# Second FFN product: from float32r pairs to plain float32 in two chunks and float16 pairs in ten

## The chip, the cores and the metric

The kernel runs on one core of one Trainium2 chip. The metric is device microseconds of one execution. Engines: TensorE (PE, with its weight loads PEld), VectorE (DVE), ScalarE (ACT), GpSimd (POOL), and SyncE (SP), whose queue issues all transfers here.

## The reference, cut to what matters

A local attention with block summaries feeds a feed-forward network (FFN):

```python
# q, k, v: (4, 8, 768, 64) float
k_sum = k.reshape(B, H, nb, 32, D).max(axis=3); v_sum = ....mean(axis=3)
scores_l = scale * q @ k^T, kept where |i - j| < 16
scores_s = scale * q @ k_sum^T + log(32)
a = softmax(concat(scores_l, scores_s))
x = a @ concat(v, v_sum)            # as (3072 tokens, 512)
h = x @ w_in                        # 512 -> 2048
g = h / (1 + exp(-h))
out = g @ w_out                     # 2048 -> 512, 3072 x 512
```

The inputs arrive as 64-bit floats; the kernel gets the weights as pairs of 32-bit words and makes float32 of them itself.

## The kernel before, in words

**Tiling.** The 3072 tokens are 24 stages of 128 (attention, six for each of four batch entries) and 12 chunks of 256 (FFN). The FFN's hidden dimension of 2048 is 8 weight pairs (`fp`) of 256. One item is one chunk with one weight pair: first product (`ffn1`, L749), 24 float16 matmuls of 128x256 (x and w_in are each a high and a low float16, three of the four cross products are taken); `tanh` (L761) and a gate (L762); then `g` is split into `gh` (L763) and `gl` (L764, in helper L228); then the second product (`ffn2`, L756), 2 halves of 6 matmuls of 128x512, in float32r (also high and low, three cross products). Chunks 0 and 1 run first, interleaved over the weight pairs: chunk 0 pairs 0 to 3, chunk 1 pairs 0 to 7, chunk 0 pairs 4 to 7. Chunks 2 to 11 follow in order with all eight pairs each.

**Weights** (`job_w`, L672). There are 16 weight tiles of 1 MB in memory (8 pairs, `kind` 0 is w_in, `kind` 1 is w_out), each loaded once by L681 into its own buffer `wr`, in which early attention data lie before. ScalarE takes the upper words (L689) into a staging buffer `raw`, ScalarE or VectorE prepares the lower words (L685, L687), VectorE joins them (L691, into `raw`). For `kind` 0 a maximum (L696), two tiny matmuls (L700, L701) and L704 give a power-of-two scale `u` and its inverse `r`. Then a scaled high half (L720, in helper L218) and the low remainder (L722, in helper L225) are written, float16 for w_in and float32r for w_out. `asc` combines the weight scale with the scale of v for the `tanh`.

**Scale of v** (`v_scale`, L408). Per batch entry, ScalarE sums absolute values (L436; L513 for the first), VectorE adds these up (`am_sum`, L405), and the largest of 128 partitions becomes a power of two.

**Attention.** For each stage four head groups: scores (L575 plain float32 for the first batch entry, L577 and L578 float16 later), softmax, the probabilities as float16 pairs `p` (L624), a transposing transfer (L627), and the product with v (L656); the first two stages run in plain float32 (L609 to L641). `job_mean` makes the block means with plain float32 matmuls (L509). `job_x` (L669, L670) writes x as `xh` and `xl`.

**Order.** All of this is handed to a planner (`Plan`), which has a cost for each operation on each engine that can run it, latencies and due times (`prio`, with offsets from `TUNE`). It simulates the engines, picks engine and order, and the kernel issues instructions in that order; each engine works through its list in order. While TensorE has nothing to do before the FFN starts, the plan puts filler matmuls (L312) there.

Of the kernel before, what the change touches and what calls it, by code (L numbers as in the profile page):

```python
# [19 lines left out]
DM, DFF = 512, 2048  # L20
# [30 lines left out]
NSUP = 2  # L51

# [151 lines left out]
def local_attn_ffn(ctx: ExitStack, tc: tile.TileContext, qkT, qF, qD, kF, kD, v, vR, w, out):  # L204
# [33 lines left out]
    wt = {}  # L238
    wr = [wp.tile([P, 2, DM, 2], U32, name="wt") for _ in range(2 * NFP)] if wide else None
# [9 lines left out]
    nc.vector.memset(spread, 2.0 ** -13)  # L249
# [7 lines left out]
    asc_t = [const.tile([P, NFP], F32, name=f"asc{i}") for i in range(2)]  # L257

# [48 lines left out]
    gh_t = ring(NG, [P, 2 * CH], F32R, "gh")  # L307
    gl_t = ring(NG, [P, 2 * CH], F32R, "gl")
# [96 lines left out]
    def am_sum(n, prio):  # L405
        plan.op({"dve": 73}, lambda e: nc.vector.tensor_reduce(out=am_t[:, 7:8], in_=am_t[:, :n], axis=AX.X, op=ALU.add), r=[("am", j) for j in range(n)], w=["am4"], prio=prio)

    def v_scale(b, prio):  # L408
# [7 lines left out]
            lambda e: nc.vector.tensor_scalar(out=sc2[:, 1:2], in0=sc2[:, 1:2], scalar1=2.0 ** -14, scalar2=None, op0=ALU.mult),  # L416
# [7 lines left out]
        if b:  # L424
            plan.op({"pool": 250, "dve": 150}, lambda e: times(e, asc_t[b % 2], ur_t[:, :, 0], vsc_t[b % 2][:, 1:2]),
                    r=[("vsc", b % 2)] + [("ur", f) for f in range(NFP)], w=[("asc", b % 2, f) for f in range(NFP)], prio=prio)

    def job_v(b, prio):
        prio += nudge("v", b)
        for j in range(4):  # L430
# [5 lines left out]
            plan.op({"act": 830}, lambda e, vr=vr, j=j: nc.scalar.activation(out=vr, in_=vr, func=AF.Abs, accum_out=am_t[:, j:j + 1]), r=[("vm", j)], w=key + [("am", j)], prio=prio)  # L436
# [60 lines left out]
    def job_mean(prio):  # L497
        prio += nudge("mean")
        k = sbank()
        for t in range(NTILE):  # L500
# [10 lines left out]
            if NPL < NTILE:  # L511
                junk, jk = pinned()
                plan.op({"act": 612}, lambda e, src=src, t=t, junk=junk: nc.scalar.activation(out=junk[:, :DM], in_=src, func=AF.Abs, accum_out=am_t[:, t:t + 1]), r=key, w=jk[:1] + [("am", t)], prio=prio)  # L513
# [41 lines left out]
    def job_a(m, prio):  # L555
# [24 lines left out]
        plan.op({"pe": 640 if b == 0 else 330}, scores, r=[(x, s % 2, hp) for x in ("qk", "qkm") for hp, _ in heads(g)] + ([("qkk", s % 2)] if b else []), w=[("bank", k)], prio=prio, cols=728)  # L580
# [91 lines left out]
    def job_w(fp, kind, prio):  # L672
        prio += nudge("w", fp, kind)
        (wf, key), src = low_staging(), w[fp, kind]
        mine = [("w", f, kind) for f in (2 * fp, 2 * fp + 1)]
        if wide:
            rt = wr[2 * fp + kind].rearrange("p j c i -> p (j c) i")
            low, top = rt[:, :, 0], rt[:, :, 1]
            wu = wf.bitcast(U32)
            sides = [k + x for k in mine for x in ((0,), (1,), (0, "side"), (1, "side"))]  # L680
            plan.op({"dma": 3300}, lambda e: nc.sync.dma_start(out=rt.rearrange("p c i -> p (c i)"), in_=src.bitcast(U32)), w=mine + sides, prio=prio - TUNE["w_dma"] + nudge("wd", fp, kind))  # L681
# [7 lines left out]
            plan.op({"act": 1000}, lambda e: nc.scalar.activation(out=wf, in_=top.bitcast(F32), func=AF.Prelu, scale=REBIAS, alpha=-SIGN), r=mine, w=key, prio=prio)  # L689
            plan.op({"act": 1000, "dve": 610}, last_bits, r=mine, w=[("wb", fp, kind)], prio=prio)  # L690
            plan.op({"dve": 1140}, lambda e: nc.vector.scalar_tensor_tensor(out=wu, in0=wu, scalar=3, in1=low, op0=ALU.logical_shift_left, op1=ALU.bitwise_or), r=mine + [("wb", fp, kind)], w=key, prio=prio)  # L691
        else:
            plan.op({"dma": 1650}, lambda e: nc.sync.dma_start(out=wf, in_=src), w=key + mine, prio=prio)
        u, r = ur_t[:, fp, 0:1], ur_t[:, fp, 1:2]
        if kind == 0:
            plan.op({"dve": 1160}, lambda e: nc.vector.tensor_reduce(out=wm_t[:, fp:fp + 1], in_=wf, axis=AX.X, op=ALU.max, apply_absolute_value=True), r=key, w=[("wm", fp)], prio=prio, port=())  # L696
            k = sbank()

            def gather(e):
                nc.tensor.matmul(out=bank[k][:, :2], lhsT=spread, rhs=wm_t[:, fp:fp + 1].to_broadcast([P, 2]), start=True, stop=False)  # L700
                nc.tensor.matmul(out=bank[k][:, :2], lhsT=spread, rhs=least.to_broadcast([P, 2]), start=False, stop=True)  # L701

            plan.op({"pe": 240}, gather, r=[("wm", fp)], w=[("bank", k)], prio=prio, cols=2)
            plan.op({"dve": 170}, lambda e: nc.vector.scalar_tensor_tensor(out=ur_t[:, fp, :].bitcast(U32), in0=bank[k][:, :2].bitcast(U32), scalar=0x7F800000, in1=flip, op0=ALU.bitwise_and, op1=ALU.bitwise_xor),  # L704
                    r=[("bank", k)], w=[("ur", fp)], prio=prio, port=())
            plan.op({"pool": 250, "dve": 130}, lambda e: times(e, asc_t[0][:, fp:fp + 1], u, vsc_t[0][:, 1:2]), r=[("ur", fp), ("vsc", 0)], w=[("asc", 0, fp)], prio=prio)
        by = u if kind else r

        def flat(part):
            return wt[fp, kind][:, part].rearrange("p j c -> p (j c)")  # L710

        def hi(e):
# [21 lines left out]
    def job_f(i, c, f):  # L734
# [30 lines left out]
        for u in range(2):  # L765
            plan.op({"pe": 1380}, ffn2(u), r=[("gh", n), ("gl", n), have[1], have[3], ("wl", f, 1)], w=[("bank", ob[u])] + ([("turn", i)] if u else []), prio=late, cols=3072)
# [151 lines left out]
```

## Time and profile before

| | |
|---|---|
| median of the runs | 668.44 us (667.22, 668.44, 670.69) |
| profiled execution | 665.93 us, span 664.1 us |
| TensorE busy | 643.0 us, 97% of the span |
| VectorE, ScalarE, GpSimd busy | 470.9, 409.0, 208.9 us |
| granted TensorE clock | 0.997 |
| TensorE, L749 (both forms) | 2304 matmuls |
| TensorE, L756 (both forms) | 1152 matmuls |
| moved by DMA | 97.39 MB, mean 147 GB/s |

The span runs from the first to the last instruction of the profiled execution; the execution's own time is 1.8 us longer. Matmuls overlap in the record, so the mean of one matmul's length is not its price: the price is the distance from start to start. In the rows, `bank<-wt,gh 128*128 128x512` means: PSUM tile `bank`, written from `wt` and `gh`, a stationary 128x128 against a moving 128x512.

### The profile page before, as it was taken

The page shows a single profiled execution, that of the slowest core. Times are in us where ns is not written, and L with a number is a line of the kernel's source. Part 1 is how long each engine was busy: PE and PEld are TensorE (multiplying, and loading weights), DVE is VectorE, ACT ScalarE, POOL GpSimd, SP SyncE. Part 2 cuts the span into 40 slices and gives each one's busy share as a digit, 9 for nine tenths or more (in the row PEclk, how much of TensorE's full clock was granted, in tenths as well). Part 3 has the DMA queues.
Part 4 walks back from the last instruction along what each step waited for, and adds up shares of the span by engine and source line. Part 5 has one row for each costly group of instructions (what it writes and reads, how often), then busy time and mean ns, then how long its engine had stood idle before and what let it go on. Part 6 is the DMA issues. An engine that isn't in the chain of part 4 may idle for free. (4 is left out here: it accounts for less than half of the span.)

```text
span 664.1 us, 13776 instructions
## 1 busy us (share of the span) xinstructions
PE 643.0 (97%) x5032; PEld 513.5 (77%) x5032; DVE 470.9 (71%) x1354; ACT 409.0 (62%) x892; POOL 208.9 (31%) x218
## 2 busy tenths in 40 slices
PE   7999799998999999999999999999999999999997
PEld 2667578776887888878887887887788888888886
DVE  5998778768679975778898955598883658843221
ACT  5898697766577665567665754467863647533222
POOL 3025565313543352124246123233442332100000
PEclk9999899999999999999999999999999999999999
DMA  8697871687564785465764764256663352310000
GB/s 285 247 327 226 315 277 56 156 203 192 140 145 120 171 210 170 112 163 121 194 134 121 198 171 148 69 149 148 157 181 98 91 133 42 78 37 13 33 1 32
DMA packets 99239, 97.39 MB, mean 147 GB/s; under 512 B 76887, under 2 KB 79959, under 8 KB 97123
## 3 DMA queue, kind: packets, MB, share of 16 engines
q1 hardware_dynamic: 99170, 96.51, 53.0%
q8 instruction: 39, 0.64, 0.4%
q14 instruction: 30, 0.24, 0.1%
HBM read 70.34 MB, written 6.29 MB: 115 GB/s over the span
## 5 line engine op out<-in xcount | busy, mean ns | idle before, releaser
L749 PE MATMUL bank<-xh,wt 128*128 128x256 f16 x1536 | 272.8, 274 | 2.3 <-DVE wt L225 2.0
L749 PEld LDWEIGHTS <-wt 128*128 128x128 f16 x2304 | 218.3, 98 | 51.1 <-issue 23.7
L756 PE MATMUL bank<-wt,gh 128*128 128x512 f32 x768 | 249.8, 406 | 0.3 <-ACT gh L763 0.3
L749 PE MATMUL bank<-xl,wt 128*128 128x256 f16 x768 | 210.1, 274 | 0.0
L756 PE MATMUL bank<-wt,gl 128*128 128x512 f32 x384 | 152.0, 396 | 4.7 <-POOL gl L228 4.6
L756 PEld LDWEIGHTS bank<-wt,gh 128*128 128x128 f32 x768 | 134.8, 189 | 25.5 <-issue 0.8
L228 POOL TENSOR_TENSOR gl<-t,gh 128x512 fp32r<-128x512 f32 x59 | 86.3, 1463 | 187.9 <-ACT gh L763 154.6
L762 DVE SCALAR_TENSOR_TENSOR t<-t,bank 128x512 f32<-128x512 f32 x96 | 65.6, 683 | 73.8 <-ACT t L761 73.3
L761 ACT ACTIVATE t<-bank,asc 128x512 f32<-128x512 f32 x96 | 65.3, 682 | 83.0 <-PE bank L749 82.6
L624 DVE SCALAR_TENSOR_TENSOR p<-e,sum,p 128x128 f16<-128x128 f32 x352 | 101.6, 350 | 6.7 <-ACT p L596 4.3
L585 ACT ACTIVATE e<-e,mx 128x182 f32<-128x182 f32 x192 | 83.7, 437 | 26.8 <-DVE mx L582 26.5
L756 PEld LDWEIGHTS bank<-wt,gl 128*128 128x128 f32 x384 | 72.0, 188 | 24.5 <-POOL gl L228 8.0
L763 ACT CAST gh<-t 128x512 fp32r<-128x512 f32 x96 | 58.9, 614 | 37.5 <-DVE t L762 35.0
L582 DVE CUSTOM_DVE_ANT_0 e<-bank,masks,qsc 128x182 f32<-128x182 f32 x144 | 52.8, 400 | 19.1 <-PE bank L578 18.8
L598 POOL TENSOR_SCALAR p<-e,sum 128x182 f16<-128x182 f32 x66 | 30.7, 471 | 112.7 <-DVE sum L591 55.9
L228 POOL TENSOR_TENSOR vv<-raw,vv 128x1024 f16<-128x1024 f32 x19 | 42.0, 2211 | 12.3 <-ACT vv L210 10.1
L228 DVE TENSOR_TENSOR gl<-t,gh 128x512 fp32r<-128x512 f32 x37 | 31.9, 863 | 17.0 <-ACT gh L763 16.6
L596 ACT ACTIVATE p<-e,sum 128x182 f16<-128x182 f32 x74 | 30.5, 439 | 19.9 <-DVE sum L591 9.5
L585 ACT ACTIVATION_READ_ACCUMULATOR e<-e,mx 128x1 f32 x192 | 36.1, 188 | 0.0
L481 DVE SCALAR_TENSOR_TENSOR qk<-raw,qsc,qk 64x1264 f16<-64x1264 f32 x18 | 30.1, 1669 | 6.9 <-ACT qk L480 6.4
L656 PEld LDWEIGHTS <-vv 128*64 128x64 f16 x880 | 25.6, 110 | 6.2 <-issue 4.8
L480 ACT ACTIVATE qk<-raw,qsc 128x1264 f16<-128x1264 f32 x18 | 24.2, 1343 | 8.9 <-DMA raw<-in_kD_dram 8.9
(133 smaller groups left out, 685.9 us busy)
## 6 DMA issues: line engine op xcount, KB each, us to landing
wt<-in_w_dram SPq DMA_DIRECT2D x16, 1024.0 KB
raw<-in_kD_dram SPq DMA_DIRECT2D x18, 632.0 KB
raw<-in_v_dram SPq DMA_DIRECT2D x20, 512.0 KB
raw<-in_qD_dram SPq DMA_DIRECT2D x18, 512.0 KB
out_dram<-raw SPq DMA_DIRECT2D x24, 256.0 KB
raw<-in_kF_dram SPq DMA_DIRECT2D x12, 384.0 KB
raw<-in_qF_dram SPq DMA_DIRECT2D x9, 512.0 KB
raw<-in_vR_dram SPq DMA_DIRECT2D x12, 384.0 KB
```

Source lines behind the costliest of these rows:

```text
L228: eng[e].tensor_tensor(out=out, in0=in0, in1=in1, op=ALU.subtract)
L481: plan.op({"dve": 1450}, lambda e: nc.vector.scalar_tensor_tensor(out=kst[64:, :, :NLOC], in0=kr[64:], scalar=qs[64:, 1:2], in1=kst[64:, : ...
L582: plan.op({"dve": 258 if b == 0 else 323}, lambda e, i=i: nc.vector.tensor_tensor_reduce(out=et[:, i, :], in0=sc[:, i, :NKEY], in1=mask, s ...
L585: plan.op({"act": 431}, lambda e, i=i, h=h: nc.scalar.activation(out=et[:, i, :], in_=et[:, i, :], func=AF.Exp, scale=-1.0, bias=mx[:, i:i ...
L596: nc.scalar.activation(out=out, in_=et[:, i, :], func=AF.Copy, scale=by)
L598: nc.gpsimd.tensor_scalar(out=out, in0=et[:, i, :], scalar1=by, scalar2=0.0, op0=ALU.mult, op1=ALU.add)
L624: nc.vector.scalar_tensor_tensor(out=pt[:, i, to:to + z - a], in0=et[:, i, a:z], scalar=su[:, i:i + 1], in1=pt[:, i, a:z], op0=ALU.mult, o ...
L749: nc.tensor.matmul(out=h[:, d * CH:(d + 1) * CH], lhsT=wt[f, 0][:, part, d, ct * P:(ct + 1) * P], rhs=x[:, ct, :], start=(ct == 0 and q == ...
L756: nc.tensor.matmul(out=bank[ob[u]], lhsT=g[:, d * CH + u * P:d * CH + u * P + P], rhs=wt[f, 1][:, part, d, :], start=(opens and d == 0 and ...
L761: plan.op({"act": 590}, lambda e: nc.scalar.activation(out=t, in_=h, func=AF.Tanh, scale=asc_t[c // 3 % 2][:, f:f + 1]), r=[("bank", k), ( ...
L762: plan.op({"dve": 605}, lambda e: nc.vector.scalar_tensor_tensor(out=t, in0=t, scalar=1.0, in1=h, op0=ALU.add, op1=ALU.mult), r=[("bank", ...
L763: plan.op({"act": 515}, lambda e: nc.scalar.copy(out=gh, in_=t), r=[("t", j)], w=[("gh", n)], prio=at - TUNE["post"])
```

## The change

- `ffn2` of chunks 0 and 1 (`NPW = 2`): one plain float32 matmul per weight block instead of three float32r ones, with `g` scaled by `u` on ScalarE and the joined float32 w_out as it is. No split of `g` or of w_out is needed for them.
- `ffn2` of chunks 2 to 11: the same three cross products, but `gh`, `gl` and both halves of w_out are float16. Their scale must be common to all eight pairs: a new `job_wo` waits for the sums of absolute values of all eight w_out tiles (a new ScalarE Abs with a sum in each), makes one power of two `kap`, and a new `split_w` then splits the eight w_out tiles. The output scale becomes `osc`.
- The joining of the weights' words is done in the weight tile itself; the `raw` staging buffers are no longer used for it. The float16 halves take the tile's other half.
- The scale of v comes from maxima of absolute values, on VectorE, in place of sums on ScalarE.
- Scales' constants, the planner's costs of the touched operations, and the offsets in `TUNE` differ.

```diff
+NPW = 2
...
-    gh_t = ring(NG, [P, 2 * CH], F32R, "gh")
-    gl_t = ring(NG, [P, 2 * CH], F32R, "gl")
+    g_t = ring(NG, [P, 2 * CH], F32, "g")
...
+    def out_scale(b, prio):
+        plan.op({"pool": 250, "dve": 130}, lambda e: times(e, osc_t[b % 2], kap_t[:, 1:2], vsc_t[b % 2][:, 1:2]), ...)
...
@@ job_v
-            plan.op({"act": 830}, lambda e, vr=vr, j=j: nc.scalar.activation(out=vr, in_=vr, func=AF.Abs, accum_out=am_t[:, j:j + 1]), ...)
+            plan.op({"dve": 869}, lambda e, vr=vr, j=j: nc.vector.tensor_reduce(out=am_t[:, j:j + 1], in_=vr, axis=AX.X, op=ALU.max, apply_absolute_value=True), ...)
...
@@ job_mean
-                plan.op({"act": 612}, ... nc.scalar.activation(out=junk[:, :DM], in_=src, func=AF.Abs, accum_out=am_t[:, t:t + 1]), ...)
+                plan.op({"dve": 603}, ... nc.vector.tensor_reduce(out=am_t[:, t:t + 1], in_=src, axis=AX.X, op=ALU.max, apply_absolute_value=True), ...)
...
@@ job_w
+        home = wr[2 * fp + kind].rearrange("p j c i -> p (j c i)")
+        wu = home[:, :2 * DM]
+        wf = wu.bitcast(F32)
...
-            plan.op({"act": 1000}, ... nc.scalar.activation(out=wf, in_=top.bitcast(F32), func=AF.Prelu, ...)
-            plan.op({"dve": 1140}, ... nc.vector.scalar_tensor_tensor(out=wu, in0=wu, scalar=3, in1=low, ...)
+            plan.op({"act": 1040}, ... nc.scalar.activation(out=top.bitcast(F32), in_=top.bitcast(F32), func=AF.Prelu, ...)
+            plan.op({"dve": 1200}, ... nc.vector.scalar_tensor_tensor(out=wu, in0=top, scalar=3, in1=low, ...)
...
+        if kind:
+            plan.op({"act": 1040}, ... nc.scalar.activation(out=home[:, 2 * DM:].bitcast(F32), in_=wf, func=AF.Abs, accum_out=wo_t[:, fp:fp + 1]), ..., prio=prio + TUNE["wo"])
+            return
...
+    def split_w(fp, kind, by, need, prio):
+        hi, lo = (wt[fp, kind][:, i].rearrange("p j c -> p (j c)") for i in range(2))
+        plan.op({"act": 1050}, lambda e: times(e, hi, wf, by), ...)
+        plan.op({"dve": 1250}, lambda e: rest_of(lo, wf, by, hi), ...)
+
+    def job_wo(prio):
+        plan.op({"dve": 75}, lambda e: nc.vector.tensor_tensor(out=wo_t, in0=wo_t, in1=ur_t[:, :, 0], op=ALU.mult), ...)
...
+        plan.op({"pool": 250, "dve": 75}, lambda e: times(e, uk_t, ur_t[:, :, 0], kap_t[:, 0:1]), ...)
+        out_scale(0, prio)
...
@@ job_f
+            terms = ((g, plain_w[f, 1]),) if plain else ((gh, wt[f, 1][:, 0]), (gh, wt[f, 1][:, 1]), (gl, wt[f, 1][:, 0]))
+                    for q, (a, b) in enumerate(terms):
+                        nc.tensor.matmul(out=bank[ob[u]], lhsT=a[:, d * CH + u * P:d * CH + u * P + P], rhs=b[:, d, :], ...)
...
+        if plain:
+            plan.op({"act": 600}, lambda e: times(e, g, t, ur_t[:, f, 0:1]), ...)
+        else:
+            plan.op({"act": 540}, lambda e: nc.scalar.copy(out=gh, in_=t), ...)
+            plan.op({"pool": 1280, "dve": 640}, lambda e: less(e, gl, t, gh), ...)
...
+            plan.op({"pe": 1720 if plain else 1300}, ffn2(u), ...)
...
+    job_wo(need_c[NPW] - TUNE["kap"])
+    for f in range(NFP):
+        split_w(f, 1, uk_t[:, f:f + 1], ["uk"], need_c[NPW] + 2 * f - TUNE["kap"])
```

More of the change, by code (lines that the diff above doesn't have):

```diff
@@ L237, in local_attn_ffn @@
     wide = w.dtype == mybir.dt.int64
-    wt = {}
-    wr = [wp.tile([P, 2, DM, 2], U32, name="wt") for _ in range(2 * NFP)] if wide else None
+    wt, plain_w = {}, {}
+    wr = [wp.tile([P, 2, DM, 2], U32, name="wt") for _ in range(2 * NFP)]
     def raw_w(f, kind):
@@ L694, in job_w @@
         u, r = ur_t[:, fp, 0:1], ur_t[:, fp, 1:2]
[L695 to L712, printed above, removed]
-            if kind:
-                wt[fp, kind] = wp.tile([P, 2, 2, DM], F32R, name="wt")
-            else:
-                home = wr[2 * fp].rearrange("p j c i -> p (j c i)") if wide else wp.tile([P, 2 * DM], U32, name="wt")
-                wt[fp, kind] = home.bitcast(F16)[:, :4 * DM].rearrange("p (i j c) -> p i j c", i=2, j=2)
-            times(e, flat(0), wf, by)
@@ new lines, in job_w, with gather @@
+        if kind:
+            plan.op({"act": 1040}, lambda e: nc.scalar.activation(out=home[:, 2 * DM:].bitcast(F32), in_=wf, func=AF.Abs, accum_out=wo_t[:, fp:fp + 1]), r=whole, w=[("wp", fp, kind), ("wo", fp)], prio=prio + TUNE["wo"])
+            return
+        plan.op({"dve": 1160}, lambda e: nc.vector.tensor_reduce(out=wm_t[:, fp:fp + 1], in_=wf, axis=AX.X, op=ALU.max, apply_absolute_value=True), r=whole, w=[("wm", fp)], prio=prio, port=())
+        k = sbank()
+        def gather(e):
+            nc.tensor.matmul(out=bank[k][:, :2], lhsT=spread, rhs=wm_t[:, fp:fp + 1].to_broadcast([P, 2]), start=True, stop=False)
+            nc.tensor.matmul(out=bank[k][:, :2], lhsT=spread, rhs=least.to_broadcast([P, 2]), start=False, stop=True)
@@ L737, in job_f @@
         k, j, n, z = nxt("h", 2) if c < NSUP else nxt("late h", 3), i % NT2, i % NG, slot[c]
-        h, t, gh, gl = bank[k], t_t[j], gh_t[n], gl_t[n]
+        h, t, g = bank[k], t_t[j], g_t[n]
+        gh, gl = (g.bitcast(F16)[:, i * 2 * CH:(i + 1) * 2 * CH] for i in range(2))
+        plain = c < NPW
         xh, xl = xh_t[z], xl_t[z]
@@ L752, in ffn2 @@
         def ffn2(u):
+            terms = ((g, plain_w[f, 1]),) if plain else ((gh, wt[f, 1][:, 0]), (gh, wt[f, 1][:, 1]), (gl, wt[f, 1][:, 0]))
             def go(e):
                 for d in range(2):
-                    for q, (g, part) in enumerate(((gh, 0), (gh, 1), (gl, 0))):
-                        nc.tensor.matmul(out=bank[ob[u]], lhsT=g[:, d * CH + u * P:d * CH + u * P + P], rhs=wt[f, 1][:, part, d, :], start=(opens and d == 0 and q == 0), stop=(closes and d == 1 and q == 2))
+                    for q, (a, b) in enumerate(terms):
+                        nc.tensor.matmul(out=bank[ob[u]], lhsT=a[:, d * CH + u * P:d * CH + u * P + P], rhs=b[:, d, :], start=(opens and d == 0 and q == 0), stop=(closes and d == 1 and q == len(terms) - 1))
@@ L757, in ffn2 @@
             return go
         for d in range(2):
[L760 to L761 removed]
+            plan.op({"pe": 1310}, ffn1(d), r=[(x, z, half) for x in ("xh", "xl") for half in range(2)] + [("wh", f, 0), ("wl", f, 0)] + ([("turn", i - APART)] if i >= APART else []), w=[("bank", k)], prio=at + nudge("f1", i), cols=3072)
@@ L797, in job_stage @@
         if s == 0:
-            plan.op({"pool": 1}, lambda e: None, w=["mask"], prio=-90.0)
+            plan.op({"pool": 1}, lambda e: None, w=["mask"] + [("qkk", i) for i in range(2)], prio=-90.0)
             job_k(0, -74)
```

89 lines of the change are left out of this document (62 added, 27 removed).

## The prediction

> **What bounds the kernel now.** I read the summary first, then the busy time by stage, then the rows of TensorE, then what it waited for. Columns of the stage table: stretch, its length, busy time of each engine with its instructions, granted TensorE clock, share of the DMA engines, GB/s.
>
> ```profile
> span 664.1 us, 13776 instructions
> PE 643.0 (97%) x5032; PEld 513.5 (77%) x5032; DVE 470.9 (71%) x1354; ACT 409.0 (62%) x892; POOL 208.9 (31%) x218
> ...
> 0.00:53.70 53.70, 48.60 (x320) 30.44 (x321) 44.02 (x192) 40.51 (x115) 12.39 (x34) 1.00 0.84 277
> 53.70:95.00 41.30, 36.01 (x296) 28.32 (x293) 30.86 (x32) 34.09 (x40) 23.26 (x16) 0.96 0.84 304
> 95.00:168.00 73.00, 71.33 (x510) 56.61 (x509) 56.47 (x140) 51.82 (x103) 27.72 (x27) 1.00 0.58 150
> 168.00:500.00 332.00, 327.00 (x2674) 266.54 (x2675) 261.27 (x771) 212.91 (x488) 122.88 (x124) 1.00 0.59 150
> 500.00:664.00 164.00, 160.07 (x1240) 131.64 (x1238) 78.30 (x222) 69.70 (x150) 22.68 (x18) 1.00 0.23 56
> ```
>
> TensorE is busy for 97% of the span. From 95 us to the end it misses only 1.7 + 5.0 + 3.9 us, the last of which is mostly the final output copy. There a TensorE nanosecond is a nanosecond of the run. Before 53.70, where the first FFN matmul (L749) starts, TensorE also runs filler matmuls (L312), so its busy time says little, and VectorE (44.02) and ScalarE (40.51) set the pace. Between 53.70 and 95 it is idle for 5.3 us, and its clock averages 0.96, which is another 0.04 x 41.3 = 1.7 us. Adding the 1.7 us idle from 95 to 168 gives 8.7 us that the first two chunks lose. What TensorE waited for (us in total, times, longest):
>
> ```profile
> PE bank L756 <- POOL gl L228: 4.6, 5, 1.5
> PE bank L749 <- DVE wt L225: 2.0, 1, 2.0
> ...
> PE bank L700 <- DVE wm L696: 1.4, 2, 1.1
> ...
> PE bank L756 <- POOL gl L228: 1.3, 2, 1.0
> ```
>
> The wait on `wt` L225 is for the low half of a weight pair, that on L696 for the maximum of a weight, that on `gl` for the low half of the gated activation (the last row is the same wait counted up to 140 us only: 1.3 of 4.6). These ends of chains lie on VectorE, ScalarE and GpSimd, not on a transfer.
>
> **The change, term by term.**
>
> *1. Ten chunks with float16 pairs (TensorE, on the path).* The count of second-product matmuls stays: 10 chunks x 8 weight pairs x 2 halves x 6 = 960 of 128x512. From the chain of waits, where columns are start, length, what:
>
> ```profile
> 637.24 5.26 PE bank L749 x48
> 642.49 5.48 PE bank L756 x24
> 647.98 5.26 PE bank L749 x48
> 653.23 6.86 PE bank L756 x30
> ```
>
> Today one costs 6.86/30 = 228.7 ns. A float16 one of 256 columns costs 5.26/48 = 109.6 ns. A second float16 length gives the slope; of a run of eight score matmuls of 182 columns, the second and the last:
>
> ```profile
> 445.92 0.24 PE L578 MATMUL bank<-qk 128*128 128x182 f16 x1
> ...
> 446.39 0.24 PE L578 MATMUL bank<-qk 128*128 128x182 f16 x1
> ```
>
> (446.39 - 445.92)/6 = 78.3 ns, so (109.6 - 78.3)/74 = 0.42 ns per column, and 512 columns are 109.6 + 256 x 0.42 = 217 ns. The gain is 960 x 11.7 ns = **-11.2 us**. Ends: two 256-column ones end to end, 219.2 ns, give -9.1; 212 ns (the slope with 0.01 us of rounding on the row) gives -16.
>
> *2. Two chunks in plain float32 (TensorE).* 2 x 8 x 2 halves x 2 = 64 matmuls take the place of 192, which cost 192 x 228.7 = 43.9 us. Plain float32 of 128x512 is in the trace in the block means (24 weight columns); each is recorded as two passes:
>
> ```profile
> 11.78 1.04 PE L509 MATMUL bank<-wt,blocks 128*24 128x512 f32 x2
> 12.75 1.05 PE L312 MATMUL bank<-ident 128*128 128x256 bf16 x8
> 13.72 1.04 PE L509 MATMUL bank<-wt,blocks 128*24 128x512 f32 x2
> 14.69 0.88 PE L575 MATMUL bank<-qk 64*128 64x182 f32 x4
> ```
>
> From start to the next start it is 0.97 us. That includes the weight load of the matmul behind it, which in a stream is covered. Four times 512 columns at 0.417 ns would be 0.855. I take 0.87, near the low end, since four such passes follow each other in a half and the present float32r weights are loaded under matmuls nearly entirely (228.7 against 217 although a load is 189 ns, row below). 64 x 0.87 = 55.7: **+11.8 us**; ends 0.855 (+10.8) and 0.97 (+18.2).
>
> ```profile
> L756 PEld LDWEIGHTS bank<-wt,gh 128*128 128x128 f32 x768 | 134.8, 189 | 25.5 <-issue 0.8
> L575 PEld LDWEIGHTS bank<-qk 64*128 64x128 f32 x96 | 14.2, 186 | 6.9 <-issue 2.1 <-ACT qk L210 1.3 <-POOL qk L212 0.8
> ```
>
> So TensorE's own sum is +0.6 us, between -5 and +9. The time is decided by the slack.
>
> *3. The early conversions (53.70 to 168).* Rows of what leaves and what replaces it, and, last, the busy time of L756 alone in the early stretch (TensorE, weight loads):
>
> ```profile
> L228 POOL TENSOR_TENSOR gl<-t,gh 128x512 fp32r<-128x512 f32 x59 | 86.3, 1463 | 187.9 <-ACT gh L763 154.6
> L763 ACT CAST gh<-t 128x512 fp32r<-128x512 f32 x96 | 58.9, 614 | 37.5 <-DVE t L762 35.0
> L689 ACT ACTIVATE raw<-wt 128x1024 f32<-128x1024 f32 x16 | 18.3, 1144 | 0.8 <-DVE wt L225 0.8
> L685 ACT ACTIVATE wt<-wt 128x1024 uint32<-128x1024 uint32 x14 | 15.9, 1140 | 5.4 <-DMA wt<-in_w_dram 5.4
> L691 DVE SCALAR_TENSOR_TENSOR raw<-raw,wt 128x1024 uint32<-128x1024 uint32 x16 | 20.3, 1271 | 4.6 <-ACT raw L689 4.4
> L218 ACT ACTIVATE wt<-raw,ur 128x1024 fp32r<-128x1024 f32 x8 | 9.2, 1146 | 0.4 <-DVE raw L691 0.4
> L365 ACT ACTIVATE raw<-raw 128x1024 f32<-128x1024 f32 x9 | 9.5, 1054 | 4.8 <-DMA raw<-in_qF_dram 4.8
> L365 ACT ACTIVATION_READ_ACCUMULATOR raw<-raw 128x1 f32 x9 | 1.7, 187 | 0.0
> L225 DVE SCALAR_TENSOR_TENSOR wt<-raw,ur,wt 128x1024 fp32r<-128x1024 f32 x8 | 13.5, 1683 | 1.4 <-ACT wt L218 1.4
> ...
> 53.70:95.00 41.30, 14.51 (x54) 9.46 (x54) 0.96 0.84 304
> ```
>
> For each of the eight second weights, 1.68 us of VectorE (L225, float32r) and a ScalarE scaling of 1.15 us leave the road to the first use; the second weight is usable as soon as L691 is done. All 16 `gl` of 1.46 us vanish with no successor; `gh` becomes one scaled copy of the same size (0.61). The added Abs with a sum on ScalarE (1.05 + 0.19, the q rows of L365) is off the path by its own priority, and takes the place of the scaling. Converting in place changes strides, not sizes: L685 already writes with a stride, at 1140 against 1144 ns contiguous, so L689 and L691 keep their prices. It also drops two staging buffers' waits; the 16 weight loads on SP's queue stay, and each waits for what lay in its tile, as before. An item is both products of one weight pair for one chunk, with 12 matmuls L756 today; 54/12 = 4.5 items pass their second product before 95. Each is to be 0.74 us longer (11.8/16), so 3.3 us of term 2 fall into a stretch in which TensorE stood still or ran slow for 7.0 us anyway, and the lighter chains give part of the rest. I take **-5.6 us**; ends 0 (the weights' DMA, 0.84 busy here, sets the pace) and -8.7 (all of it).
>
> *4. Maxima in place of sums for v.* ScalarE loses 12 x (842 + 187) and 6 x (624 + 187) ns = 17.2 us, VectorE gains 12 x 0.95 (priced by the v reduction over the same 768 elements) + 6 x 0.61 (half the 1024-wide row below) = 15 us.
>
> ```profile
> L434 DVE TENSOR_REDUCE vm<-raw 128x24 f32<-128x768 f32 x12 | 11.4, 948 | 4.2 <-DMA raw<-in_vR_dram 4.2
> L696 DVE TENSOR_REDUCE wm<-raw 128x1 f32<-128x1024 f32 x8 | 9.7, 1212 | 0.1
> L513 ACT ACTIVATE raw<-wt 128x512 f32<-128x512 f32 x6 | 3.7, 624 | 3.9 <-DMA wt<-in_v_dram 3.9
> L436 ACT ACTIVATE raw<-raw 128x768 f32<-128x768 f32 x12 | 10.1, 842 | 9.2 <-DVE vm L434 8.8 <-ACT e L585 0.3
> L413 DVE TENSOR_REDUCE sc<-bank 1x1 f32<-1x128 f32 x4 | 1.1, 274 | 0.2 <-PE bank L410 0.2
> ```
>
> Eight of the twelve fall into 168 to 500, where VectorE has 71 us free: nothing. Six come at 3 to 16 us; VectorE is not full then but is later in the prologue, and there the low half of the first second weight (L225) leaves it: I take 0 for the start of the FFN, ends -2 and +2.
>
> *5. The postponed split.* After the last Abs comes a chain of some ten VectorE instructions of at most 0.27 us (the like of L413, the longest) and two small matmuls, then 8 x 1.15 us on ScalarE and 8 x 1.7 us at most on VectorE, before the second product of chunk 2. With four of the v maxima, VectorE gets some 8 x 1.6 + 4 x 0.95 + 1 = 18 us more between about 100 and 180; it has 73.0 - 56.5 = 16.5 free up to 168, and the stretch grows by about 8. ScalarE has 21 free for 9. Three of the moved low halves lie in this stretch today and leave it:
>
> ```profile
> 96.98 2.05 DVE L225 SCALAR_TENSOR_TENSOR wt<-raw,ur,wt 128x1024 fp32r<-128x1024 f32 x1 [0.18 <-ACT wt L218]
> ...
> 117.93 1.94 DVE L225 SCALAR_TENSOR_TENSOR wt<-raw,ur,wt 128x1024 fp32r<-128x1024 f32 x1 [0.28 <-ACT wt L218]
> ```
>
> So VectorE finds about 16.5 + 8 + 6 us for 18. GpSimd's five tiny scalings are nothing at 31% load. **0**; end +5. On the engines, what stands behind a split that waits for `uk` is the tanh and gate of the next item, and TensorE after them: this is the price if the cover fails.
>
> Sum: -11.2 + 11.8 - 5.6 + 0 + 0 = -5.0 us. The profiled run took 665.93 us (span 664.1), 2.5 below the median of 668.44; against it the sum gives 660.9, and against the median, which I predict, **663.4**.
>
> **Rivals.** A change below 0.5% (3.3 us) cannot be told from none here.
>
> *A. The slack does not pay.* Weights arrive no sooner, since the loads wait on the attention tiles in their buffers, and what the plain product loses in one item is lost in the next. For it: DMA 0.84 busy; against it: the three waits shown end on VectorE and GpSimd, none on a weight's DMA. Then +0.6: 669.0. Same. 0.22.
>
> *B. The postponed split is late.* In order on VectorE and ScalarE, it holds up gate work, and TensorE runs dry at the start of chunk 2. Eight splits in series are 8 x 1.5 = 12 us; TensorE is two items (2 x 5.2 us) ahead only on the first product. A stall of 10 us gives 673.4; from 8.4 us on (668.4 + 0.5% less 663.4) the change is slower. Against it: the free time in term 5. Chance 0.10.
>
> *C. Float32 weight loads stay uncovered.* Each pass would carry its 189 ns: 64 x (0.855 + 0.378) = 78.9 us, 23.2 more than in term 2, so 686.6. Against it: 228.7 ns in a stream whose loads are 189 could not be if they were exposed. 0.03.
> The Trainium skill, "TensorE: Matmul & The Clock Gate", section "The mechanism", says that weight loads overlap running matmuls only if their row group differs, which full 128-row weights never do. By that rule this rival would hold; the trace's 228.7 ns disagrees for float32r, and only the plain form remains untested.
>
> *D. The float16 matmul is no cheaper at 512 columns*, because something else than the weight load makes the 228.7. Term 1 is 0: 674.6. The slope of term 1 speaks against. 0.05.
>
> *E. All slack and the low prices.* -16 + 10.8 - 8.7 - 2 = -15.9: 652.5. 0.10.
>
> **How the numbers follow.** My forecast has 0.50; its own range, with the terms' nearer halves, is 659 to 667, of which I give 0.43 to more than 0.5% faster (below 665.1). Faster: 0.43 + E 0.10 = 0.53. Same: 0.07 + A 0.20 = 0.27 (A with the high end of term 2 spills 0.02 over). Slower: 0.02 + B 0.10 + C 0.03 + D 0.05 = 0.20. The range to leave out about 2 in 10 is 656 to 672: it drops most of E, B, C and D.
>
> **What would show it.** Float16 second products at 217 ns in a row of 24 or 30; plain ones at 0.87 from start to start; TensorE idle between the first FFN matmul and the end of chunk 1 near 3 us and its clock near 1.00; no wait of TensorE on the postponed halves; the first FFN matmul near 53.7. A float32 stream above 0.97, a gap of several us ahead of chunk 2, or the same idle time as today would make it wrong.

## The result, and the profile after

The changed kernel takes 639.68 us (median; 637.46 to 642.86), the kernel before 667.83 beside it: ratio 0.9575, interval 0.9524 to 0.9625. A second set of runs gave 641.49 us, ratio 0.9608 (0.9576 to 0.9640). The prediction was 663.4, with a range of 656 to 672: right in sign, 24 us too high, and the time lies below the range. The medians below leave out one slow execution of e5 (659.90 us).

The profiled execution after took 642.86 us, 3 above its median; the one before (665.93) lay 2 under its own. So the profiles differ by 23.1 us where the medians differ by 28.2. The top of the page after, then its stage table (columns as in the prediction):

```profile
span 641.1 us, 13605 instructions
PE 629.0 (98%) x4940; PEld 425.8 (66%) x4940; DVE 467.8 (73%) x1365; ACT 407.6 (64%) x895; POOL 178.9 (28%) x200
```

```profile
0.00:52.30 52.30, 48.05 (x337) 29.25 (x337) 45.10 (x177) 37.78 (x106) 14.37 (x33) 1.00 0.84 270
52.30:95.00 42.70, 42.02 (x283) 28.01 (x280) 38.17 (x55) 40.66 (x56) 14.04 (x14) 1.00 0.91 317
52.30:165.02 112.72, 112.04 (x702) 71.15 (x699) 95.42 (x212) 88.97 (x152) 27.98 (x31) 1.00 0.68 215
165.02:641.10 476.08, 468.89 (x3909) 325.43 (x3906) 327.24 (x977) 280.84 (x639) 136.61 (x138) 1.00 0.49 124
```

The last two rows are the first two chunks (up to the first matmul of chunk 2) and the ten others. The same two stages of the kernel before:

```profile
53.70:168.20 114.50, 107.54 (x806) 85.11 (x803) 87.33 (x171) 86.11 (x142) 50.98 (x43) 0.99 0.67 205
168.20:664.10 495.90, 486.88 (x3911) 397.99 (x3910) 339.57 (x992) 282.41 (x637) 145.56 (x142) 1.00 0.47 119
```

So the prologue became 1.4 us shorter, the first two chunks 1.8, the ten chunks 19.8. In the first two chunks TensorE has 4.5 us more busy time (112.04 against 107.54) and 6.3 less idle time (0.68 against 6.96), and its clock is no longer below 1.00. In the ten chunks 18.0 of the 19.8 are busy time. What TensorE still waits for after (us, times, longest), and its second products, which now have two prices:

```profile
PE bank L522 <- DMA wt<-in_v_dram: 2.8, 2, 1.8
...
PE bank L790 <- ACT g L800: 1.1, 1, 1.1
PE bank L790 <- DVE g L232: 0.7, 1, 0.7
PE bank L790 <- ACT g L222: 0.7, 2, 0.5
PE bank L790 <- POOL g L232: 0.6, 1, 0.6
```

```profile
615.26 5.18 PE bank L790 x24
...
630.90 6.49 PE bank L790 x30
```

No row of the whole list names a w_out half: TensorE does not wait for the postponed split. The second fence is from the chain of waits: 6.49/30 = 216 ns for a float16 matmul of 512 columns (217 was predicted).

### The profile page after: what moved, and what is told of

Same layout as the page of the kernel before. It is cut to its first block, busy times and chain, and to the rows that moved or that the text cites. A ratio compares the mean times of both kernels' runs of the same rounds, so it can differ in the third digit from the quotient of the medians.

```text
span 641.1 us, 13605 instructions
## 1 busy us (share of the span) xinstructions
PE 629.0 (98%) x4940; PEld 425.8 (66%) x4940; DVE 467.8 (73%) x1365; ACT 407.6 (64%) x895; POOL 178.9 (28%) x200
## 4 chain that ended last, share of the span: by engine, by line
PE 65%; DVE 12%; ACT 8%; DMA 8%; issue 3%; SPq 2%; POOL 2%; POOLq 0%; DVEq 0%; ACTq 0%
PE bank L790 29%; PE bank L781 27%; DVE p L636 4%; DMA raw<-in_v_dram 2%; PE bank L668 2%; PE bank L587 2%; DVE qk L494 2%; DMA raw<-vms 2%; DMA raw<-in_kD_dram 2%; ACT wt L704 2%; DVE e L594 1%; PE bank L589 1%; PE bank L590 1%; PE bank L522 1%; DMA wt<-in_w_dram 1%
## 5 line engine op out<-in xcount | busy, mean ns | idle before, releaser
L790 PE MATMUL bank<-wt,g 128*128 128x512 f16 (+1 forms) x1088 | 283.2, 405 | 3.1 <-ACT g L800 1.1
L781 PEld LDWEIGHTS <-wt 128*128 128x128 f16 x2304 | 224.1, 98 | 43.0 <-issue 5.0
L790 PEld LDWEIGHTS <-g 128*128 128x128 f16 x960 | 91.9, 98 | 96.2 <-DVE g L232 1.6
L232 POOL TENSOR_TENSOR g<-t,g 128x512 f16<-128x512 f32 x41 | 53.0, 1293 | 101.8 <-ACT g L800 101.7
L610 POOL TENSOR_SCALAR p<-e,sum 128x182 f16<-128x182 f32 x72 | 40.4, 567 | 142.1 <-DVE sum L603 42.1
L800 ACT CAST g<-t 128x512 f16<-128x512 f32 x80 | 49.2, 615 | 41.6 <-DVE t L796 40.4
L232 DVE TENSOR_TENSOR g<-t,g 128x512 f16<-128x512 f32 x39 | 32.8, 840 | 21.2 <-ACT g L800 21.1
L608 ACT ACTIVATE p<-e,sum 128x182 f16<-128x182 f32 x89 | 36.4, 439 | 13.8 <-DVE sum L603 5.2
L790 PEld LDWEIGHTS bank<-wt,g 128*128 128x128 f32 x128 | 22.5, 190 | 23.2 <-issue 20.3
L589 PE MATMUL bank<-qk 128*128 128x182 f16 x144 | 27.7, 242 | 0.0
```

The source lines that it names most:

```text
L232: eng[e].tensor_tensor(out=out, in0=in0, in1=in1, op=ALU.subtract)
L610: nc.gpsimd.tensor_scalar(out=out, in0=et[:, i, :], scalar1=by, scalar2=0.0, op0=ALU.mult, op1=ALU.add)
L781: nc.tensor.matmul(out=h[:, d * CH:(d + 1) * CH], lhsT=wt[f, 0][:, part, d, ct * P:(ct + 1) * P], rhs=x[:, ct, :], start=(ct == 0 and q == ...
L790: nc.tensor.matmul(out=bank[ob[u]], lhsT=a[:, d * CH + u * P:d * CH + u * P + P], rhs=b[:, d, :], start=(opens and d == 0 and q == 0), sto ...
L800: plan.op({"act": 540}, lambda e: nc.scalar.copy(out=gh, in_=t), r=[("t", j)], w=[("gh", n)], prio=at - TUNE["post"])
```

## The experiments

A plain measure helps in this section. Executions of one kernel vary by several us, and the longer ones have the lower mean granted clock: over the 60 executions of the kernel before that ran beside these experiments, with spans of 662.0 to 672.2 us and clocks of 0.997 to 0.982, the correlation is -0.87, and span times clock stays within 657.7 to 663.7. I call that product the clock-free span; it removes the time lost at half clock while TensorE is busy.

| kernel | median us | ratio to before (95%) | clock-free span, median |
|---|---|---|---|
| before | 666 to 670 | 1 | 661.0 |
| after, two sets | 639.68, 641.49 | 0.9575, 0.9608 | 637.8, 639.4 |
| e2 float16 pairs alone, order of before | 656.92 | 0.9805 (0.9742 to 0.9868) | 646.7 |
| e5 the same, another order | 653.49 | 0.9733 (0.9655 to 0.9811) | 643.0 |
| e11 the same, a third order | 648.12 | 0.9700 (0.9665 to 0.9734) | 641.3 |
| e9 after, another order | 646.36 | 0.9684 (0.9638 to 0.9729) | 643.8 |
| e10 after, a third order | 648.09 | 0.9714 (0.9672 to 0.9755) | 645.3 |
| e15 before, another order | 666.94 | 1.0000 (0.9975 to 1.0025) | 659.5 |
| e16 before, a third order | 665.75 | 0.9984 (0.9962 to 1.0005) | 661.3 |
| e12 before, planner's price raised | 675.31 | 1.0112 (1.0065 to 1.0159) | 668.3 |
| e4 after, offsets of before | 664.49 | 0.9923 (0.9887 to 0.9960) | 655.9 |
| e3 after, early work back, order kept | 679.76 | 1.0139 (1.0081 to 1.0196) | 671.9 |
| e6 after, early `gl` back, refitted | 657.60 | 0.9809 (0.9759 to 0.9859) | 653.6 |
| e7 after, early split back, refitted | 654.61 | 0.9766 (0.9708 to 0.9825) | 652.2 |
| e8 after, sums for v back, refitted | 651.37 | 0.9723 (0.9669 to 0.9776) | 644.5 |
| e13 after, float32r pairs back | 655.41 | 0.9825 (0.9792 to 0.9858) | 653.3 |
| e17 after, first two chunks' second product as float16 | 636.48 | 0.9540 (0.9513 to 0.9566) | 634.7 |

"Refitted" means that the offsets in `TUNE` were searched again for that kernel by the planner's own planned end.

### What a pair's type is worth: e1 and e13

e1 has only matmul streams: 24 float16 128x256 matmuls and then 12 of float32r (L45), 12 of float16 (L49) or 8 passes of plain float32 (L53), eight times each; the same behind attention products (L36) and scores; then long streams.

> A stream of TensorE matmuls alone, no FFN: groups are repeated eight times each, and their period is read from start to start. Theory P (the prediction's price of a float32r matmul, 228.7 ns, holds only inside a stream; each group of them pays extra where it follows float16 work): 24 float16 of 256 columns and 12 float32r of 512 take 5.43 to 5.48 us, with 12 float16 of 512 they take 5.21, with 4 plain float32 6.05 to 6.1; 40 products of attention and 6 float32r take 0.2 to 0.3 us more than with 6 float16; 8 scores and 6 float32r 0.1 more than with 6 float16. Theory S (the stream prices are all there is, and the rest of the gain is in waits): 5.37 against 5.22, and 0.07 us for each of the other two pairs.

```profile
24.44 2.76 PE bank L45 x12
27.20 2.64 PE bank L30 x24
...
67.45 2.59 PE bank L49 x12
70.03 2.62 PE bank L30 x24
...
109.97 3.44 PE bank L53 x8
113.41 2.62 PE bank L30 x24
...
150.98 1.59 PE bank L45 x6
152.57 1.24 PE bank L36 x40
...
175.05 1.24 PE bank L36 x40
176.28 1.40 PE bank L49 x6
...
225.40 10.91 PE bank L45 x48
236.31 10.38 PE bank L49 x48
246.69 13.75 PE bank L53 x32
```

In long streams float32r costs 227.3 ns, float16 216.3, a plain pass 429.7 (a plain matmul 0.859 us). But an item of the FFN has groups: 24 + 12 takes 5.40 us with float32r and 5.21 with float16, a difference of 0.19 us where twelve matmuls of the streams differ by 0.13. A float32r group costs some 0.06 us extra where it follows other work, which I call its entry. Behind attention products six matmuls and their lead-in take 1.59 + 1.24 = 2.83 us against 1.40 + 1.24 = 2.64; there the entry is 0.19 less 0.07, or 0.12 us. Behind eight scores the period is 2.07 against 1.92 us, an entry of 0.08. The first two differences lie between the two theories, the third (0.15) is above both. By the first, 80 x 0.19 = 15.2 us, which is above the 11.2 of the prediction.

e13 asks the program itself. It keeps the order and all of the other work of the changed kernel; the moving side of the ten chunks is a filled tile, so TensorE reads no split halves there (it waits for none in the changed kernel either).

```diff
+    gr_t = ring(NG, [P, 2, 2 * CH], F32R, "g")
+    wr32 = const.tile([P, DM], F32R, name="wr32")
...
-        gh, gl = (g.bitcast(F16)[:, i * 2 * CH:(i + 1) * 2 * CH] for i in range(2))
+        gh, gl = (gr_t[n][:, i] for i in range(2))
...
+            terms = ... if plain else ((gh, wr32), (gh, wr32), (gl, wr32))
```

> The changed kernel in its own order, with the pairs of its ten chunks in float32r again: the stationary halves are float32r, and the moving side is a filled float32r tile in place of the w_out halves, whose splitting still runs. Everything else, the order on each engine too, is as in the changed kernel. Theory T (the pairs' type is worth what the ten chunks lost, 80 items x 0.235 us between the items' lengths of 5.475 and 5.24): 639.7 + 19 = 659, between 656 and 662. Theory P (the price that the prediction used, 11.7 ns for each of 960 matmuls): 651. Theory O (the order and the lighter early work carry the change): 645 or less.

Its stage table (first two chunks, ten chunks) and a row of its chain of waits:

```profile
49.87:161.99 112.12, 111.66 (x703) 71.25 (x699) 92.90 (x212) 88.51 (x152) 28.34 (x31) 1.00 0.69 218
161.99:651.60 489.61, 485.29 (x3909) 399.50 (x3906) 330.57 (x977) 282.72 (x639) 140.29 (x138) 1.00 0.47 121
```

```profile
641.08 6.84 PE bank L792 x30
```

The type alone is worth 14 to 16 us: 655.41 against 639.68 and 641.49, or 653.3 against 637.8 and 639.4 free of clock. That is just under theory T's 656 to 662, above P's 651, and far from O's 645. The rows say how it comes about. TensorE's busy time in the ten chunks is 485.29 against 468.89: 16.4 us of work. The matmuls themselves give 960 x (6.84 - 6.49)/30 = 11.2 us, exactly the prediction's term. The other 5.2, or 0.065 per item, are of the size of the entries in e1 (0.06 for a group of 12); that they are these entries is concluded, not measured one by one. And idle time went the other way: 4.3 us here, 7.2 in the changed kernel, so that 13.5 of the 16.4 reach the stage's length. I read this as the faster product leaving the gate chain less time.

### Float16 pairs alone: e2, e5, e11

The kernel before with float16 halves for both sides in all twelve chunks, and nothing else of the change. The scale stays one per weight pair and isn't brought to a common one.

```diff
-    gh_t = ring(NG, [P, 2 * CH], F32R, "gh")
-    gl_t = ring(NG, [P, 2 * CH], F32R, "gl")
+    gh_t = ring(NG, [P, 2 * CH], F16, "gh")
+    gl_t = ring(NG, [P, 2 * CH], F16, "gl")
...
-        by = u if kind else r
+        by = r
```

> The kernel before with one thing altered: both halves of w_out and of the gate are float16 instead of float32r, in all 12 chunks, with each weight pair's own scale (the pairs' scales are not brought together, so the output is scaled differently per pair). Order and offsets stay those of before. Theory P: 0.23 us for each of 80 items, 18.6 us, and little in the first two chunks, which wait for other things: 646 to 651. Theory S: 0.14 us per item, 11 to 13 us: 655 to 657. Theory O (the new order and offsets carry most of it): not below 655.

> The kernel before with float16 pairs in the second product of all 12 chunks (each pair's own scale, so the output is scaled differently per pair), as in the earlier run, with the planner told the float16 price (1300 in place of 1380) and its offsets searched anew, by its own planned end, for this set of operations. All early conversions of before remain: w_out is split before its first use, every item has its remainder, no matmul is plain. Theory D (the dtype's price, with an order that fits it, is nearly the whole gain, and the plain product in the first two chunks about pays for itself): 641 to 647. Theory W (the work taken off the road to the first two chunks is at least a third of it): 650 or more, since that work is all still there.

> The kernel before with float16 pairs in all chunks (per-pair scales, so the output is scaled differently per pair), refitted from another random start. Theory D (dtype and fitted order are nearly all): within 3 us of the other orders of the changed kernel. Theory W (the early work taken off is worth something of its own): 5 us or more above them, and 650 to 658.

Free of clock the three orders stand at 646.7, 643.0 and 641.3, a mean of 643.7: 17 us under the mean of the three orders of before (660.6). In their medians they gain less: e2 (656.92) lies where theories S and O had it and e5 (653.49) where W had it; only e11 (648.12) lies where D had it. The difference is half clock: in the median execution it takes 7.5, 6.5 and 4.5 us from them, and 0.3, 0.0 and 1.0 us from the three orders of the changed kernel. In e5, TensorE waits longest where the prediction found it waiting in the kernel before, only longer:

```profile
PE bank L754 <- ACT gh L761: 7.5, 6, 3.4
PE bank L754 <- POOL gl L228: 6.5, 7, 1.7
```

### Order alone: e9, e10, e15, e16, e12, e4

Only the offsets differ, for instance:

```diff
-TUNE = dict(km=71.68, w_dma=-32.42, w_dec=-108.83, ...)
+TUNE = dict(km=766.94, w_dma=184.07, w_dec=-249.35, ...)
```

> The changed kernel, every operation the same, with other offsets found by a fresh search from a random start, so another order of nearly equal planned end. Theory L (which order is taken matters by itself, and the changed kernel's is a good one): 644 to 652, with more half-clock stretches than the changed kernel. Theory N (any fitted order does about the same): 638 to 643.

> As the run before it, from another random start. Theory L: 641 to 650. Theory N: 638 to 642. The two together give the spread that an order alone makes, against which the 12 to 18 us of the runs with early work or sums put back are to be read.

> The kernel before, the same operations in another order (other offsets, found by search from a random start by the planner's own estimate). Theory D (order spreads a kernel over some 8 us; the change itself is worth what the means over orders differ by, some 20 us): 660 to 676. Theory L (the order of before was an unlucky one, and the change gained mostly a better order): 655 or less.

> As the run before, a third order of the kernel before. Theory D: 660 to 676, so that the mean over three orders of before stays 18 to 25 us above the mean over three orders of the changed kernel (644.7). Theory L: 655 or less.

> The kernel before, every operation the same, with the planner told 1455 instead of 1380 for half a second product, which is what it takes between other work, and its offsets refitted. If before lost time because its plan ran ahead of the chip: span times granted clock below 657 (the kernel before has 661) and 655 to 662 in all. If not: 666 to 671.

> The changed kernel with the planner's offsets of the kernel before (the two new ones stay). Theories P and C: the ten chunks cost the same per item, the start may move by a few us either way: 636 to 646. Theory O: most of the 28 us goes: 652 or more.

Two other fitted orders of the kernel before are no faster than its own, so the change did not gain merely by leaving an unlucky order. The traces say so too. What TensorE lost in the first two chunks (one profiled execution each, from the first FFN matmul to the first of chunk 2):

| | idle, us | at half clock, us lost |
|---|---|---|
| before, e15, e16 | 7.0, 8.7, 4.7 | 1.7, 3.4, 0 |
| float16 alone: e2, e5, e11 | 9.3, 4.5, 9.2 | 5.1, 0, 5.1 |
| after, e9, e10 | 0.7, 2.0, 0.0 | 0, 0, 0 |
| e4 | 9.3 | 5.1 |

Under each of three fitted orders of the changed kernel nearly all of this loss is gone; under none of the three with float16 alone is it. Two other orders of the changed kernel are 5 to 8 us slower than its own: the shipped order is a good one of its kind. e12 tells the planner the measured price of the float32r group; the one order that was found with it is 1.1% slower, so nothing shows that a wrong price held the kernel before back. It also shows that a single refit of the same operations can come out 7 to 9 us higher free of clock (668.3 against 659.5 to 661.3). e4 runs the changed operations under the old offsets, and nearly all of the gain is gone, as theory O had it:

```profile
49.35:176.50 127.15, 117.83 (x732) 74.29 (x730) 89.36 (x203) 91.33 (x148) 28.44 (x35) 0.96 0.61 187
176.50:661.10 484.60, 472.44 (x3915) 326.29 (x3913) 344.01 (x986) 282.08 (x631) 149.75 (x149) 1.00 0.48 123
```

Its ten chunks have the cheap pairs (472.44 busy), but 12.2 us idle, and its first two chunks take 127 us. An edit of this size can't be judged under offsets that were fitted to other work.

### The early work and the plain product: e3, e6, e7, e8, e17

e3 adds to the changed kernel an early split of each w_out tile and a `gl` for each plain item, both unused; e6 adds the `gl` alone and e7 the split alone, with refitted offsets. e8 puts the ScalarE sums for v back.

```diff
+            plan.op({"act": 1050}, lambda e: times(e, eh, wf, u), ...)
+            plan.op({"dve": 1250}, lambda e: rest_of(el, wf, u, eh), ...)
...
+            plan.op({"pool": 1280, "dve": 640}, lambda e: less(e, spill, t, g), ...)
```

> The changed kernel with the conversions that it took off the road to the first two chunks put back, as dead weight: each w_out tile is split (ScalarE and VectorE) before its first use, and each plain item has a remainder of 128x512 on GpSimd or VectorE before its second product. The matmuls stay plain. If the first two chunks gained because these conversions left (theory C), the stretch from the first FFN matmul to the start of chunk 2 grows by 5 to 8 us, and the time to 645 to 649. If the transfers or the new order set the pace there (theory O), it stays within 2 us of the changed kernel, near 640.

> The changed kernel with a dead remainder of 128x512 on GpSimd or VectorE put back before the second product of each of the 16 plain items; offsets searched anew for this set. If those 16 operations (about 21 us on GpSimd) hold up the first two chunks: 645 to 651. If they lie beside TensorE: 638 to 643.

> The changed kernel with a dead split of each w_out tile (8 x 1.15 us on ScalarE, 8 x 1.3 to 1.7 us on VectorE) put back before its first use, beside the late split that stays; offsets searched anew. If VectorE and ScalarE set the pace up to chunk 2: 10 to 14 us more than the changed kernel, 650 to 655. If transfers or TensorE do: 638 to 644.

> The changed kernel with the scale of v taken again from ScalarE's sums instead of VectorE's maxima; offsets searched anew. All theories: within 4 us of the changed kernel, 638 to 644, since 15 us on VectorE and 17 us on ScalarE trade places in stretches where both have room. A time above 646 would make the maxima a cause of their own.

e3 is far above every theory: its first FFN matmul comes at 74.6 us, 22 late, while the first two chunks take 114.4 us, only 1.7 more. The work was pushed into an order that was made without it; that is again a result on order, not a price. Refitted, the kernel with `gl` is 9 us above the other two orders of the changed kernel (mean 644.5) and the one with the split 8, free of clock. One order was tried of each, and e12 shows that one refit alone can differ by as much, so the stages must decide. Those of e6:

```profile
0.00:56.70 56.70, 53.26 (x369) 34.83 (x369) 48.65 (x190) 41.67 (x111) 16.12 (x37) 1.00 0.88 271
56.70:170.30 113.60, 111.70 (x698) 70.88 (x694) 95.87 (x188) 88.02 (x147) 42.52 (x40) 1.00 0.68 202
170.30:653.60 483.30, 470.86 (x3915) 325.60 (x3914) 331.36 (x981) 281.71 (x644) 142.49 (x142) 1.00 0.48 122
```

The added `gl` all belong to the first two chunks, and these take 113.60 us, 0.9 more than in the changed kernel; the rest of the difference lies ahead of them and in the ten chunks, where nothing was added. So e6 shows no price of `gl`. The stages of e7:

```profile
0.00:58.15 58.15, 54.34 (x380) 35.47 (x381) 51.13 (x188) 44.51 (x112) 13.15 (x35) 1.00 0.91 292
58.15:178.15 120.00, 114.51 (x737) 72.47 (x735) 95.76 (x205) 95.27 (x158) 29.77 (x26) 1.00 0.61 176
```

Here the difference lies where the work was added: 6 us ahead of the FFN and 7 in the first two chunks, 4.8 of them as more idle TensorE (5.5 against 0.7).

e8 stands at 644.5 free of clock, as the other two orders do. But its median, 651.37, is 3 to 5 us above theirs and above the 646 that its expectation set; 4.2 us of it were at half clock. So these runs do not show that sums or maxima make no difference.

e17 takes the plain product's price away. The first two chunks use three float16 matmuls per block on a filled tile, and no split is added.

```diff
-            terms = ((g, plain_w[f, 1]),) if plain else ...
+            terms = ((gh, w16),) * 3 if plain else ...
```

> The changed kernel in its own order, in which the second product of the first two chunks runs as three float16 matmuls per block too, in place of one plain float32: ScalarE writes the scaled g as float16, and the moving side is a filled float16 tile, so that no split of w_out is needed early. No other work is added. By the price of the streams (0.2157 and 0.859 us) TensorE loses 64 x 0.859 - 192 x 0.2157 = 13.6 us of work in these chunks. Theory V (TensorE bounds the first two chunks now): 626 to 630. Theory W (VectorE, ScalarE and the weights' arrival set their pace, and the plain product only fills time in which TensorE would wait): 636 to 641.

> The changed kernel once more, beside the run before on the same chip. By theory T (execution to execution it varies by its start, not by the clock) the median is 638 to 642, and its span times clock 636 to 640.

By the streams, 64 x 0.859 - 192 x 0.216 = 13.5 us of TensorE work go, yet the time falls by only 5.0 us, from 641.49 to 636.48 on the same chip. The first two chunks of e17, and the longest wait in them, which is new (for `wom`, the largest of the sums behind the common scale):

```profile
53.77:160.45 106.68, 100.94 (x764) 66.80 (x761) 91.95 (x211) 86.73 (x149) 25.97 (x28) 0.98 0.74 229
...
PE bank L742 <- DVE wom L740: 2.2, 1, 2.2
```

TensorE is busy for 11.1 us less than in the changed kernel there (100.94 against 112.04), and idle for 5.7 us against 0.7. The time lies in theory W's range: about 5 of the 13.5 us are on the path in this order, and most of the rest fills time in which TensorE would wait. Two things bound this: the order was planned for the plain product's length, and in e17 TensorE no longer reads w_out in these chunks.

### The clock: e14

A float16 stream that stops for ScalarE: four stops of each of seven lengths, then clusters of short ones.

> Only a stream of float16 128x512 matmuls, which stops for ScalarE: four stops each of seven lengths from about 0.5 to 3 us, with 48 matmuls (10.4 us) between, then four clusters of five short stops with 5 matmuls between. Theory G (the clock falls by gap): stops from about 2 us on, and clusters of shorter ones, are followed by a stretch of about 3.4 us at half clock, single stops below 1 us by none. Rival (the half-clock stretches in the kernels have another cause than TensorE's own idle time): no stretch at half clock follows any of these stops.

The granted clock changes on a grid of 3.41 us. The busy time of each engine in some of these intervals (the first number behind the comma is TensorE's, the 1.00 or 0.50 its clock), in pairs of an interval with a stop and the next one:

```profile
272.88:276.29 3.41, 1.57 (x8) 0.56 (x7) 0.00 (x0) 1.65 (x2) 0.00 (x0) 1.00 0.00 0
276.29:279.71 3.42, 3.42 (x18) 1.57 (x16) 0.00 (x0) 0.00 (x0) 0.00 (x0) 1.00 0.00 0
...
296.78:300.19 3.41, 1.38 (x7) 0.41 (x5) 0.00 (x0) 1.90 (x2) 0.00 (x0) 1.00 0.00 0
300.19:303.60 3.41, 3.20 (x8) 1.19 (x9) 0.00 (x0) 0.15 (x1) 0.00 (x0) 0.50 0.00 0
...
310.43:313.84 3.41, 2.07 (x10) 0.75 (x8) 0.00 (x0) 1.22 (x2) 0.00 (x0) 1.00 0.00 0
313.84:324.09 10.25, 9.36 (x44) 4.29 (x45) 0.00 (x0) 0.83 (x1) 0.00 (x0) 1.00 0.00 0
```

Theory G holds in part. A stop of 2.2 us is followed by half clock where it falls into one interval (1.38 busy), and is not where it straddles two (2.07 busy); two of four did. Stops of 1.8 us never were, nor the clusters of five stops of 0.5 us. The bound in this run lies between 1.38 and 1.57 us busy out of 3.41, and an interval of e2 with 1.52 (161.46 to 164.87 us) was followed by half clock too. Busy time is not all of it: ahead of the FFN, the interval of e5 from 42.34 to 45.75 us is busy throughout, mostly with small plain float32 matmuls (L641, 128x128 against 64 weight columns), and the next one is at half clock. The kernel before has the same pattern behind the 2 us wait on `wt` that the prediction quotes:

```profile
72.92:76.33 3.41, 1.13 (x8) 0.44 (x7) 2.30 (x3) 3.41 (x5) 0.00 (x0) 1.00 1.03 423
76.34:79.75 3.41, 3.41 (x19) 2.43 (x17) 3.37 (x4) 2.85 (x4) 0.47 (x1) 0.50 0.52 123
```

## Why the prediction was wrong, point by point

In the two profiles the span fell by 23.0 us, and the sum had said 5.0. Here is where they lie, with TensorE's matmuls counted from start to next start and waits left out (half clock taken off):

| us | before | after | change | predicted |
|---|---|---|---|---|
| both products, first two chunks | 90.0 | 99.7 | +9.7 | +11.8 |
| both products, ten chunks | 439.1 | 419.1 | -20.0 | -11.2 |
| idle and half clock, first two chunks | 8.7 | 0.7 | -8.0 | -5.6 |
| idle, ten chunks and end | 9.0 | 7.2 | -1.8 | 0 |
| other work of TensorE behind the prologue | 63.2 | 61.7 | -1.5 | 0 |
| prologue | 53.7 | 52.3 | -1.4 | 0 |

The step that failed is first of all TensorE's own sum, which the prediction put at +0.6 and "between -5 and +9" and which came to -10.3; the slack of term 3 adds 2.4 us, and 4.7 us lie where the prediction had nothing.

**Term 1, float16 pairs: size too small.** The price per matmul was right (11.7 ns predicted, 11.7 measured between e13 and after). It came from the tail, where groups of 24 and 30 follow each other. In the body each group of 12 or 6 pays an entry, which no term had. With only the type changed (e13), the ten chunks' products take 436.7 us against 419.1, and the other matmuls between them 1.1 less, so that float16 saves 16.4 us of TensorE's work instead of 11.2, some 14 to 16 in the time. The other 2.4 us, from 439.1 to 436.7, came with the other order.

**Term 2, plain float32: price right, sum too high.** In the kernel the plain products cost 56.7 us from start to next start (55.7 predicted); in a long stream (0.859 us each) they would cost 55.0. But the float32r groups that they replaced cost 47.6 in the trace of before, not 43.9, for the same reason as term 1: +9.1 instead of +11.8. By e1's items, 6.06 against 5.40 us, it is +10.6. e17 shows moreover that not all of what it costs is paid.

**Term 3, early conversions: too small.** Nearly all of the idle time in the first two chunks went, not part of it: 7.0 us idle and 1.7 at half clock became 0.7 and none, where the prediction named "near 3 us" idle. I added the price of term 2 to a stage and took part of its slack off as if the two were separate. They are not: where the plain product's price is taken away, 5.7 us of idle time come back (e17), and where the early split comes back, 5.5 do (e7). The longer product gives the gate chain time, and the lighter chain needs less. The stage as a whole became 1.8 us shorter where +6.2 was predicted, but 3.6 of that is work beyond its borders: 1.8 us of attention and scales now lie ahead of it and 1.75 us of plain passes behind the first matmul of chunk 2.

**Terms 4 and 5.** Term 5 is zero, as predicted: no wait on the postponed halves is in the list. Term 4 was not settled: e8 shows nothing free of clock, and 3 to 5 us in the median.

**What no term held.** The offsets in `TUNE` were named as part of the change and costed at nothing. e4 against after shows 18 us free of clock for them, and the other fitted orders show 5 to 8 us between one good order and the next. With the order free, float16 alone (mean 643.7) and the whole change (637.8 to 645.3 over three orders) are alike free of clock: the plain product and the lighter early work about pay for each other there, and the shipped order adds some 6 us. In the medians the whole change is 8 us ahead of float16 alone (mean of three orders 644.7 against 652.8), 6 of them half clock. And the median of before holds 4.0 us at half clock (span less clock-free span, median of 60 executions), of which its profiled execution shows 2.1; after has 0.3. I carried the 2.5 us between profile and median over unchanged.

By medians, of the 28.2 us about 15 are for the type (e13 against after), 8 for the rest with its order (661.0 against e13's 653.3), and 5 remain, of which the clock explains 3.7.

**The rivals.** A (the slack does not pay) and B (the split is late) fall by the stage table and the list of waits. D falls by e1 and e13. C falls by e1: a plain pass takes 429.7 ns although its weight load takes 190, so the load is covered. The sentence of the Trainium skill, "TensorE: Matmul & The Clock Gate", section "The mechanism", by which weight loads overlap running matmuls only where the row group differs, does not hold in this trace; the same section also lets a load into the background weight buffer run ahead. E (all slack, low prices, 652.5) had the right direction and was still 13 us too high. Of the signs that the prediction named, the two prices came out (216 for 217 ns, and 0.859 us in a stream or 0.886 in the kernel for 0.87); the idle time up to the end of chunk 1, 0.7 where 3 was named, is the one that showed an error.

What stays open: what makes the shipped order 6 us better than two others was not taken apart, each refit was one search, and no run prices the maxima or `gl` apart from the order.

## What to carry to other kernels

Price a matmul in the groups in which it runs, from the start of one group of its neighbours to the next, not from a long stream: the entries of float32r groups came to half as much again as their slower matmuls (5.2 us beside 11.2). In a stage where two engines feed each other, add the work per engine and ask who is last, rather than adding a price and a gain. A kernel whose order is planned must be compared with its plan fitted to it, over more than one order, before a difference of a per cent is put down to the edit.

## What the runs showed of the hardware

Short gaps cost more than their length. In e14 an interval of the 3.41 us grid in which TensorE was busy for 1.38 us or less was followed by one at half clock, which costs up to 1.7 us more (half of 3.41); where the same gap of 2.2 us fell across two intervals it cost nothing more. This fits the executions of before, which spread over 10 us with the clock, and the changed kernel, which lost its long gaps and has a clock of 0.999 to 1.000 in all of its ten executions; these still differ by 6.6 us, for a reason that no run here shows. The Trainium skill, "TensorE: Matmul & The Clock Gate", section "What's actually happening", tells of a free-running window of about 3.4 us; the trace agrees (3.41). Its section "HAM oscillation — how this bites in real kernels" sets the limit at gaps of more than about 3.4 us; here 2.2 us were enough.
